# Folding the attention values into the three FFN weight matrices, with a written instruction order

## The chip, the cores and the metric

The kernel runs on one core of a Trainium2 chip. Its engines have instruction queues of their own and run beside each other: TensorE (PE in the profile; its weight loads are PEld), VectorE (DVE), ScalarE (ACT), GpSimd (POOL, which here mostly issues the loads) and SyncE (SP, which issues the stores). The metric is the device time of one execution in microseconds; lower is better.

## The reference

Batch 8, 8 heads, 576 tokens, head size 64, 32 memory slots; then a feed-forward network (FFN) of width 768 on all 8·576 = 4608 tokens of 512 channels. Inputs and output are float32.

```python
a = softmax(phi, axis=2)                      # per token, over 32 slots
k_m = einsum('bhsm,bhsd->bhmd', a, k)         # 32 x 64 per head
v_m = einsum('bhsm,bhsd->bhmd', a, v)
attn = softmax(0.125 * q @ k_m.T)             # 576 x 32 per head
x = concat_heads(attn @ v_m)                  # 4608 x 512
h = max(x @ w1, x @ w2, x @ w3)               # 4608 x 768
out = h @ w_out                               # 4608 x 512
```

Both kernels leave out the subtraction of the maximum before each exponential.

## The kernel before, in words

**Attention, one batch after another** (`attention_batch`). `load_batch` brings phi, k, v and q in with GpSimd's DMA queue, which also narrows them to bf16: per tensor four DMAs of two heads (`L121`, `L134`), in which a partition holds four neighbouring tokens, and a fifth for the last 64 tokens (`L127`, `L140`). ScalarE takes the exponential of phi (`L148`, `L155`); VectorE rearranges k and v into `kv_c` and q into `q_tc`. Then, for each of two groups of four heads and each of two pairs in it, TensorE contracts k and v over the tokens (`L210`), transposes q (`L234`) and the values (`L248`, `L254`), and forms the scores (`L292`) in a PSUM tile `stage`. The softmax over the 32 slots goes through three ScalarE steps on `stage`: exponential (`L300`), logarithm of the sums (`L317`, after a matmul that sums, `L309`), and the exponential of minus that (`L330`, after a matmul that spreads it, `L322`); VectorE multiplies (`L334`). Last, `L347` multiplies by the values, and `L354` writes the result transposed into `xT`, which holds all 4608 tokens in SBUF.

**The FFN, in 9 tiles of 512 tokens** (`ffn_tile`). For each of 6 slices of 128 of the 768 channels, 3 x 4 matmuls of 128x512 contract the 512 channels of x with w1, w2 and w3 (`L388`) into `acc01` (two PSUM banks) and `acc2`. ScalarE copies both to bf16 (`L396`, `L398`), VectorE takes the two maxima (`L400`, `L403`). Then 4 x 6 matmuls with w_out (`L410`), copies by ScalarE (`L418`) and stores by SP (`L427`).

A planner that knows costs puts the instructions of each engine in order; in the program's text attention stands ahead of the whole FFN, and the planner mixes the first FFN tiles into the attention. Each engine takes its instructions in that order, and semaphores hold an instruction until its inputs are there. PSUM has 8 banks of 2 KB per partition; `acc01`, `acc2` and `po2` each have one buffer.

Of the kernel before, what the change touches and what calls it, by code (L numbers as in the profile page):

```python
# [12 lines left out]

EXACT_SOFTMAX = True
# [3 lines left out]
def kernel(  # L19
# [17 lines left out]
    CMAIN = 4  # L37
    SMAIN = CMAIN * P
    TAIL = S - SMAIN
    NCH = CMAIN + 1  # L40
    csz = [P] * CMAIN + [TAIL]

    DM = H * D
    DF = moe_w1.shape[1]
    NTOK = B * S
    NPAIR = H // 2
    NGRP = H // 4
    CCH = DM // P
    FCH = DF // P
    NT = 512  # L50
    NTILES = NTOK // NT

    const_pool = ctx.enter_context(tc.tile_pool(name="const", bufs=1))
    w_pool = ctx.enter_context(tc.tile_pool(name="wpool", bufs=1))
    xt_pool = ctx.enter_context(tc.tile_pool(name="xt", bufs=1))
    batch_pool = ctx.enter_context(tc.tile_pool(name="batch", bufs=2))
    batch1_pool = ctx.enter_context(tc.tile_pool(name="batch1", bufs=1))
    grp_pool = ctx.enter_context(tc.tile_pool(name="grp", bufs=2))
    pair_pool = ctx.enter_context(tc.tile_pool(name="pairp", bufs=2))
    ffn_sb_pool = ctx.enter_context(tc.tile_pool(name="ffnsb", bufs=3))  # L60
    hT_pool = ctx.enter_context(tc.tile_pool(name="hT", bufs=2))

    pair_psum_pool = ctx.enter_context(tc.tile_pool(name="ppsum", bufs=1, space=bass.MemoryType.PSUM))
    stage_psum_pool = ctx.enter_context(tc.tile_pool(name="spsum", bufs=1, space=bass.MemoryType.PSUM))
    ffn_psum_pool = ctx.enter_context(tc.tile_pool(name="fpsum", bufs=1, space=bass.MemoryType.PSUM))

    AB0 = 0
    DEN0 = 64
    BF0 = 68
    VMT0 = 0  # L70
    QT0 = 64

    def bf16_view(ppsum):
        return ppsum[:, BF0:512].bitcast(BF16)

    ident = const_pool.tile([P, P], BF16, name="ident")
    make_identity(nc, ident)

    ones_diag4 = const_pool.tile([P, 4], BF16, name="ones_diag4")
    nc.gpsimd.memset(ones_diag4, 0.0)  # L80
    for g4 in range(4):
        nc.vector.memset(ones_diag4[32 * g4 : 32 * (g4 + 1), g4 : g4 + 1], 1.0)

    blkones = const_pool.tile([P, P], BF16, name="blkones")
    nc.gpsimd.memset(blkones, 1.0)
    nc.gpsimd.affine_select(
        out=blkones, in_=blkones, compare_op=ALU.is_ge,
        fill=0.0, base=0, pattern=[[1, P]], channel_multiplier=-M,
    )
    nc.gpsimd.affine_select(  # L90
        out=blkones, in_=blkones, compare_op=ALU.is_ge,
        fill=0.0, base=M - 1, pattern=[[-1, P]], channel_multiplier=M,
    )

    den_cols = const_pool.tile([P, 2], BF16, name="den_cols")
    nc.vector.memset(den_cols[:, 0:1], 1.0)
    nc.vector.memset(den_cols[:, 1:2], 32.0)

    w_tiles = [w_pool.tile([P, CCH, DF], BF16, name=f"w{wi}") for wi in range(3)]
    wot = w_pool.tile([P, FCH, DM], BF16, name="wot")  # L100

    def emit_weight_dmas(step):
        if step < 3:
            w_ap = (moe_w1, moe_w2, moe_w3)[step]
            src = w_ap.rearrange("(cc p) f -> p cc f", p=P)
            for cc in range(CCH):
                nc.gpsimd.dma_start(
                    out=w_tiles[step][:, cc], in_=src[:, cc]
                )
        elif step == 3:  # L110
            src = moe_w_out.rearrange("(fc p) c -> p fc c", p=P)
            for fc in range(FCH):
                nc.gpsimd.dma_start(out=wot[:, fc], in_=src[:, fc])

    xT = xt_pool.tile([P, NPAIR, NTOK], BF16, name="xT")

    def load_batch(b):
        bt = {}
        phi_t = batch1_pool.tile([P, H, NCH, M], BF16, name="phi_t")
        for hp in range(H // 2):  # L120
            nc.gpsimd.dma_start(  # L121
                out=phi_t[:, 2 * hp : 2 * hp + 2, 0:CMAIN, :],
                in_=phi[b, 2 * hp : 2 * hp + 2, 0:SMAIN, :].rearrange(
                    "h (p c) m -> p h (c m)", c=CMAIN
                ),
            )
        nc.gpsimd.dma_start(  # L127
            out=phi_t[0:TAIL, :, CMAIN, :],
            in_=phi[b, :, SMAIN:S, :].rearrange("h s m -> s h m"),
        )  # L130
        for name, src in (("k", k), ("v", v), ("q", q)):
            t = batch_pool.tile([P, H, NCH, D], BF16, name=f"{name}_t")
            for hp in range(H // 2):
                nc.gpsimd.dma_start(  # L134
                    out=t[:, 2 * hp : 2 * hp + 2, 0:CMAIN, :],
                    in_=src[b, 2 * hp : 2 * hp + 2, 0:SMAIN, :].rearrange(
                        "h (p c) d -> p h (c d)", c=CMAIN
                    ),
                )
# [46 lines left out]
    def attention_batch(b):  # L186
# [5 lines left out]
        for g in range(NGRP):  # L192
# [150 lines left out]
            for pp in range(2):  # L343
# [15 lines left out]
                )  # L359

    def out_segments(col0):
        segs = []
        col = col0
        while col < col0 + P:
            b = col // S
# [107 lines left out]
```

## Time and profile before

| what | value |
|---|---|
| time, median of 3 runs | 372.61 us (370.12 to 381.8) |
| profiled execution, first to last instruction (span) | 371.9 us |
| PE busy | 299.6 us, 81% |
| ACT busy | 203.4 us, 55% |
| DVE busy | 139.8 us, 38% |
| POOL busy | 139.4 us, 37% |
| read from HBM, written | 39.32 MB, 9.44 MB |

The profiled execution's own time is its span; the page gives no other, and the span lies 0.7 us under the median of the runs. Busy time of PE counts a matmul to its modelled end, which overlaps the start of the next, so it is no measure of peak rate. In a group's row stand the line, the engine, the operation, the tiles, the shape, the count, the busy time in us, the mean of one in ns, and the idle time ahead of them with what ended it. A matmul's row gives rows x columns of the array in use (`128*64`) and then the shape of the moving operand.

### The profile page before, as it was taken

The page shows a single profiled execution, that of the slowest core. Times are in us where ns is not written, and L with a number is a line of the kernel's source. Part 1 is how long each engine was busy: PE and PEld are TensorE (multiplying, and loading weights), DVE is VectorE, ACT ScalarE, POOL GpSimd, SP SyncE. Part 2 cuts the span into 40 slices and gives each one's busy share as a digit, 9 for nine tenths or more (in the row PEclk, how much of TensorE's full clock was granted, in tenths as well). Part 3 has the DMA queues.
Part 4 walks back from the last instruction along what each step waited for, and adds up shares of the span by engine and source line. Part 5 has one row for each costly group of instructions (what it writes and reads, how often), then busy time and mean ns, then how long its engine had stood idle before and what let it go on. Part 6 is the DMA issues. An engine that isn't in the chain of part 4 may idle for free.

```text
span 371.9 us, 4813 instructions
## 1 busy us (share of the span) xinstructions
PE 299.6 (81%) x1651; PEld 130.9 (35%) x1680; DVE 139.8 (38%) x450; ACT 203.4 (55%) x263; POOL 139.4 (37%) x236
## 2 busy tenths in 40 slices
PE   0146576878798887987897779999999999999972
PEld 0023233323343333333343423344444444444430
DVE  0456436336457456366465431221213222121310
ACT  2026645753967578287466784545454544544541
POOL 9987976774998799474000000000000000000000
PEclk9999999996999899599989999999999999999997
DMA  6999999999999999695120001303022040212204
GB/s 61 159 99 147 121 102 133 109 96 128 104 139 121 168 157 147 61 129 63 52 54 10 3 0 30 85 0 105 10 57 56 2 114 0 72 42 56 58 0 114
DMA packets 60728, 29.42 MB, mean 79 GB/s; under 512 B 29216, under 2 KB 56096, under 8 KB 60704
## 3 DMA queue, kind: packets, MB, share of 16 engines
q0 software_dynamic: 54304, 19.67, 48.1%
q1 hardware_dynamic: 6400, 9.44, 9.7%
q8 instruction: 13, 0.21, 0.2%
q14 instruction: 11, 0.09, 0.1%
HBM read 39.32 MB, written 9.44 MB: 131 GB/s over the span
## 4 chain that ended last, share of the span: by engine, by line
PE 59%; ACT 12%; issue 4%; DVE 4%; DMA 4%; POOL 3%; ACTq 0%; DVEq 0%; POOLq 0%
PE acc L388 33%; PE po L410 12%; ACT L317 3%; PE stage L347 3%; PE ppsum L210 3%; PE stage L292 2%; DVE attn_g L334 2%; DMA k_t<-in_k_dram 2%; ACT eln L330 2%; ACT lncs L317 2%; PE ppsum L234 2%; ACT L330 2%; DMA wot<-in_moe_w_out_dram 2%; PE stage L322 1%; ACT h L396 1%
## 5 line engine op out<-in xcount | busy, mean ns | idle before, releaser
L388 PE MATMUL acc<-xT,w 128*128 128x512 bf16 x626 | 165.2, 392 | 5.3 <-DMA w<-in_moe_w_dram 2.1
L388 PEld LDWEIGHTS <-w 128*128 128x128 bf16 x648 | 58.9, 98 | 80.0 <-issue 20.9
L396 ACT CAST h<-acc 128x1024 bf16<-128x1024 f32 x54 | 54.6, 1011 | 53.5 <-PE acc L388 53.5
L410 PE MATMUL po<-wot,hT 128*128 128x512 bf16 x209 | 59.0, 391 | 3.4 <-ACT ost L418 1.1
L400 DVE TENSOR_TENSOR mx<-h 128x512 bf16<-128x512 bf16 x54 | 22.8, 423 | 88.3 <-ACT h L396 88.0
L210 PE MATMUL ppsum<-e_t,kv_c 128*128 128x32 bf16 (+1 forms) x320 | 24.0, 187 | 20.5 <-DVE kv_c L165 16.6
L418 ACT COPY ost<-po 128x1024 f32<-128x1024 f32 x18 | 18.2, 1009 | 32.7 <-PE po L410 26.9
L398 ACT CAST h<-acc 128x512 bf16<-128x512 f32 x54 | 31.8, 590 | 7.1 <-PE acc L388 6.9
L403 DVE TENSOR_TENSOR hT<-mx,h 128x512 bf16<-128x512 bf16 x54 | 22.9, 424 | 23.2 <-ACT h L398 19.0
L354 ACT ACTIVATE xT<-stage 128x576 bf16<-128x576 f32 x32 | 20.9, 652 | 18.7 <-PE stage L347 18.3
L210 PEld LDWEIGHTS <-kv_c 128*128 128x128 bf16 (+1 forms) x320 | 18.3, 100 | 35.5 <-DVE kv_c L165 16.8
L410 PEld LDWEIGHTS <-hT 128*128 128x128 bf16 x216 | 19.7, 99 | 29.4 <-issue 6.0
L347 PE MATMUL stage<-attn_g,vm_sb 64*128 64x512 bf16 x64 | 16.2, 342 | 14.7 <-DVE attn_g L334 13.3
L317 ACT ACT_TABLE_LOAD x16 | 20.5, 1283 | 9.0 <-PE stage L309 8.9
L121 POOL DMA_DIRECT2D phi_t<-in_phi_dram x32 | 24.8, 831 | 1.3 <-DMA wot<-in_moe_w_out_dram 0.9
L262 DVE TENSOR_SCALAR vm_sb<-ppsum,recips 32x64 bf16<-32x64 bf16 x64 | 15.8, 247 | 24.2 <-PE ppsum L254 14.9
L134 POOL DMA_DIRECT2D q_t<-in_q_dram x32 | 24.0, 780 | 0.6 <-issue 0.5
L134 POOL DMA_DIRECT2D k_t<-in_k_dram x32 | 23.7, 827 | 0.0
L134 POOL DMA_DIRECT2D v_t<-in_v_dram x32 | 23.0, 747 | 0.7 <-issue 0.6
L234 PE MATMUL ppsum<-ident,q_tc 128*128 128x128 bf16 (+1 forms) x160 | 21.0, 248 | 2.2 <-DVE q_tc L176 1.7
L196 POOL MEMSET vm_sb<- 128x128 bf16 x16 | 4.0, 254 | 46.6 <-PE stage L347 46.6
L330 ACT ACT_TABLE_LOAD x14 | 18.0, 1283 | 4.8 <-PE stage L322 4.7
(53 smaller groups left out, 265.3 us busy)
## 6 DMA issues: line engine op xcount, KB each, us to landing
out_dram<-ost SPq DMA_DIRECT2D x80, 64.0 KB, 1.7
k_t<-in_k_dram POOLq DMA_DIRECT2D x32, 128.0 KB, 4.0
v_t<-in_v_dram POOLq DMA_DIRECT2D x32, 128.0 KB, 4.3
q_t<-in_q_dram POOLq DMA_DIRECT2D x32, 128.0 KB, 4.3
out_dram<-ost SPq DMA_DIRECT2D x32, 128.0 KB, 2.4
w<-in_moe_w_dram POOLq DMA_DIRECT2D x12, 192.0 KB, 4.8
phi_t<-in_phi_dram POOLq DMA_DIRECT2D x32, 64.0 KB, 3.1
wot<-in_moe_w_out_dram POOLq DMA_DIRECT2D x6, 128.0 KB, 5.6
```

The source lines that it names most:

```text
L121: nc.gpsimd.dma_start(out=phi_t[:, 2 * hp : 2 * hp + 2, 0:CMAIN, :], in_=phi[b, 2 * hp : 2 * hp + 2, 0:SMAIN, :].rearrange("h (p c) m -> p ...
L134: nc.gpsimd.dma_start(out=t[:, 2 * hp : 2 * hp + 2, 0:CMAIN, :], in_=src[b, 2 * hp : 2 * hp + 2, 0:SMAIN, :].rearrange("h (p c) d -> p h ( ...
L210: nc.tensor.matmul(ppsum[:, AB0 + a * M : AB0 + (a + 1) * M], lhsT=kv_c[0:r, c, h, :, :], rhs=e_t[0:r, c, h, :], start=(c == 0), stop=(c = ...
L234: nc.tensor.transpose(pbf[:, QT0 + c * P : QT0 + c * P + r], q_tc[0:r, c, hA : hA + 2, :], ident[0:r, 0:r],)
L317: nc.scalar.activation(out=lncs[0:4, :], in_=stage[0:4, 0:S], func=AF.Ln, scale=1.0 / 32.0,)
L330: nc.scalar.activation(out=eln, in_=stage[:, 0:S], func=AF.Exp, scale=-1.0)
L347: nc.tensor.matmul(psum_out[:, s0:s1], lhsT=vm_sb[pp * 2 * M : (pp + 1) * 2 * M, :], rhs=mov_g[pp * 2 * M : (pp + 1) * 2 * M, s0:s1], star ...
L388: nc.tensor.matmul(tgt, lhsT=w_tiles[w][:, cc, ft * P : (ft + 1) * P], rhs=xT[:, cc, n0 : n0 + NT], start=(cc == 0), stop=(cc == CCH - 1),)
L396: nc.scalar.copy(out=h01, in_=acc01)
L398: nc.scalar.copy(out=h2, in_=acc2)
L403: nc.vector.tensor_tensor(out=hT[:, ft, :], in0=mx, in1=h2, op=ALU.max)
L410: nc.tensor.matmul(po2[:, i * DM : (i + 1) * DM], lhsT=hT[:, fc, ns * P : (ns + 1) * P], rhs=wot[:, fc, :], start=(fc == 0), stop=(fc == F ...
```

## The change

Since x @ w = attn @ (v_m @ w) head by head, the kernel after multiplies the values into the weights first. For each batch and each slice of 128 channels, `fold` forms v_m @ w for 4 heads x 32 slots = 128 rows, in two groups, and `ffn1` contracts attn over these 2 x 128 slots, where the kernel before contracted x over 4 x 128 channels. `attn @ v_m` and `xT` are gone.

The data's layout changes with it. Two heads share the 128 partitions, 64 each, and each partition holds 9 neighbouring tokens of its head: one DMA per tensor and batch (4 instead of 20), with contiguous runs of 9 x 64 numbers. phi stays float32. The exponentials of phi go into a tile that is zero outside a head's own half (`e_bd`), k, v and a block of ones lie in one tile (`kvo`), and one matmul contracts all three (`att_kv`), in two column halves of the array by `tile_position`. Scores are formed in eight tiles of 64x32 of the array (`att_score`). One matmul with a block of ones sums and spreads (`att_norm`). `fold` too uses two column halves.

A table set for ScalarE is named at the start. The maxima read PSUM directly, the first of them against `h1`, the copy of the first product. Two PSUM pools stay: `acc` with two buffers of two banks (scores, sums and FFN1 share it), `one` with four of one bank. The order is written out by hand: batch 0 goes through attention and FFN and batch 1 through attention, one step after another; from then on FFN1 of batch b, in 18 pieces, is mixed with FFN2 of batch b-1 and with the attention and folding of batch b+1, each put ahead of the piece whose number stands beside it.

```diff
--- before.py
+++ after.py
...
+    nc.scalar.preload_act_table_set("natural_log_exp_and_others")
+    ident = const.tile([P, P], BF16, name="ident")
...
+    blkones = const.tile([P, P], BF16, name="blkones")
+    nc.vector.memset(blkones, 0.0)
+    for i in range(P // M):
+        nc.vector.memset(blkones[M * i : M * (i + 1), M * i : M * (i + 1)], 1.0)
+    ones2 = const.tile([P, 2], BF16, name="ones2")
+    nc.vector.memset(ones2, 1.0)
+    e_bds, vm_bds, kvos = [], [], []
+    for i in range(2):
+        e_bd = const.tile([P, NP, NC, 2, M], BF16, name=f"e_bd{i}")
+        nc.vector.memset(e_bd, 0.0)
+        e_bds.append(e_bd)
+        vm_bd = const.tile([P, NP, 2, M], BF16, name=f"vm_bd{i}")
+        nc.vector.memset(vm_bd, 0.0)
+        vm_bds.append(vm_bd)
+        kvo = const.tile([P, 3, NP, NC, D], BF16, name=f"kvo{i}")
+        nc.vector.memset(kvo[:, 2], 1.0)
+        kvos.append(kvo)
...
+    def load(b):
+        t = {}
+        ph = inp.tile([P, NP, NC, M], FP32, name="ph")
+        kv = kvos[b % 2]
+        qq = inp.tile([P, NP, NC, D], BF16, name="qq")
+        def go(dst, src, n):
+            s = src[b].rearrange("h s d -> (h s) d").rearrange(
+                "(j p c) d -> p j (c d)", p=P, c=NC
+            )
+            nc.gpsimd.dma_start(out=dst.rearrange("p j c d -> p j (c d)"), in_=s)
+        go(ph, phi, M)
+        go(kv[:, 0], k, D)
+        go(kv[:, 1], v, D)
+        go(qq, q, D)
+        t["ph"], t["kv"], t["q"] = ph, kv, qq
+        loaded[b] = t
...
+    def att_exp(b):
+        s = st.setdefault(b, {})
+        ph = loaded[b]["ph"]
+        e_bd = e_bds[b % 2]
+        for a in range(2):
+            r = slice(HP * a, HP * (a + 1))
+            nc.scalar.activation(out=e_bd[r, :, :, a, :], in_=ph[r], func=AF.Exp)
+        s["e"] = e_bd
+    def att_kv(b, g):
+        s = st[b]
+        if g == 0:
+            s["kvp"] = one_pool.tile([P, NG, 3 * D], FP32, name="kvp", tag="one")
+        kv, e_bd, kvp = loaded[b]["kv"], s["e"], s["kvp"]
+        for c in range(NC):
+            for i in range(2):
+                j = 2 * g + i
+                nc.tensor.matmul(
+                    kvp[HP * i : HP * (i + 1), g, :],
+                    lhsT=e_bd[:, j, c],
+                    rhs=kv[:, :, j, c, :],
+                    start=(c == 0),
+                    stop=(c == NC - 1),
+                    tile_position=(0, HP * i),
+                )
+    def att_kv_norm(b):
+        s = st[b]
+        kvp = s["kvp"]
+        rden = work.tile([P, NG], FP32, name="rden")
+        nc.vector.reciprocal(out=rden, in_=kvp[:, :, 2 * D])
+        kvn = work.tile([P, NG, 2 * D], BF16, name="kvn")
+        for g in range(NG):
+            nc.vector.tensor_scalar_mul(
+                out=kvn[:, g], in0=kvp[:, g, 0 : 2 * D], scalar1=rden[:, g : g + 1]
+            )
+        s["kvn"] = kvn
+    def att_kv_t(b):
+        s = st[b]
+        kvt = one_pool.tile([P, NP, 2, M], BF16, name="kvt", tag="one")
+        for g in range(NG):
+            nc.tensor.transpose(kvt[:, 2 * g : 2 * g + 2], s["kvn"][:, g], ident)
+        kmT = work.tile([P, NP, 2, M], BF16, name="kmT")
+        for u in range(2):
+            nc.vector.tensor_copy(out=kmT[HP * u : HP * (u + 1)], in_=kvt[0:HP])
+        vm_bd = vm_bds[b % 2]
+        for a in range(2):
+            nc.vector.tensor_copy(
+                out=vm_bd[HP * a : HP * (a + 1), :, a, :], in_=kvt[HP:P, :, a, :]
+            )
+        s.update(kmT=kmT, vm=vm_bd)
+    def att_q(b, jj):
+        s = st[b]
+        qq = loaded[b]["q"]
+        if jj == 0:
+            s["qT"] = work.tile([P, NP, NCP, P], BF16, name="qT")
+        qT = s["qT"]
+        x = b % 2
+        if jj < NP // 2:
+            pt = one_pool.tile([P, 2, NCP - 1, P], BF16, name="pt", tag="one")
+            for i in range(2):
+                for c in range(NCP - 1):
+                    nc.tensor.transpose(
+                        pt[:, i, c, :], qq[:, 2 * jj + i, 2 * c : 2 * c + 2, :], ident
+                    )
+            nc.vector.tensor_copy(
+                out=qT[:, 2 * jj : 2 * jj + 2, x : x + NCP - 1, :], in_=pt
+            )
+        else:
+            pt = one_pool.tile([P, NP, P], BF16, name="pt", tag="one")
+            for j in range(NP):
+                nc.tensor.transpose(pt[0:HP, j, :], qq[:, j, NC - 1, :], ident)
+            nc.vector.tensor_copy(
+                out=qT[0:HP, :, 0 if x else NCP - 1, :], in_=pt[0:HP]
+            )
+    def att_score(b, g):
+        s = st[b]
+        kmT, qT = s["kmT"], s["qT"]
+        x = b % 2
+        if g == 0:
+            s["e2"] = work.tile([P, NG, S + HP], BF16, name="e2")
+            s["attn"] = work.tile([P, NG, S], BF16, name="attn")
+        sc = acc_pool.tile([P, 2, BANK], FP32, name="sc", tag="acc")
+        for par in range(2):
+            nch = NCP - par
+            c0 = x * par
+            r = slice(HP * par, HP * (par + 1))
+            for h4 in range(4):
+                j, a = 2 * g + h4 // 2, h4 % 2
+                nc.tensor.matmul(
+                    sc[M * h4 : M * (h4 + 1), par, 0 : nch * HP],
+                    lhsT=kmT[r, j, a, :],
+                    rhs=qT[r, j, c0 : c0 + nch, HP * a : HP * (a + 1)],
+                    start=True,
+                    stop=True,
+                    tile_position=(HP * par, M * h4),
+                )
+        for par in range(2):
+            nch = NCP - par
+            nc.scalar.activation(
+                out=s["e2"][:, g].rearrange("p (c u n) -> p c u n", u=2, n=HP)[
+                    :, 0:nch, par, :
+                ],
+                in_=sc[:, par, 0 : nch * HP].rearrange("p (c n) -> p c n", n=HP),
+                func=AF.Exp,
+                scale=0.125,
+            )
+    def att_norm(b, g):
+        s = st[b]
+        e2 = s["e2"]
+        sm = acc_pool.tile([P, 2, BANK], FP32, name="sm", tag="acc")
+        for h in range(2):
+            nc.tensor.matmul(
+                sm[:, h, 0:SH],
+                lhsT=blkones,
+                rhs=e2[:, g, h * SH : (h + 1) * SH],
+                start=True,
+                stop=True,
+            )
+        ln = work.tile([P, S], FP32, name="ln")
+        nc.scalar.activation(
+            out=ln.rearrange("p (h n) -> p h n", h=2),
+            in_=sm[:, :, 0:SH],
+            func=AF.Ln,
+        )
+        r = work.tile([P, S], FP32, name="r")
+        nc.scalar.activation(out=r, in_=ln, func=AF.Exp, scale=-1.0)
+        nc.vector.tensor_tensor(
+            out=s["attn"][:, g, :], in0=e2[:, g, 0:S], in1=r, op=ALU.mult
+        )
+    def fold(b, ft):
+        s = st[b]
+        if ft == 0:
+            s["wp"] = work.tile([P, NG, FT, 3, P], BF16, name="wp")
+        for g in range(NG):
+            wps = one_pool.tile([P, 3, P], FP32, name="wps", tag="one")
+            for i in range(2):
+                nc.tensor.matmul(
+                    wps[HP * i : HP * (i + 1)],
+                    lhsT=s["vm"][:, 2 * g + i],
+                    rhs=w_sb[:, 2 * g + i, :, ft * P : (ft + 1) * P],
+                    start=True,
+                    stop=True,
+                    tile_position=(0, HP * i),
+                )
+            if g == 0:
+                nc.scalar.copy(out=s["wp"][:, g, ft], in_=wps)
+            else:
+                nc.vector.tensor_copy(out=s["wp"][:, g, ft], in_=wps)
+    def ffn1(b, ft, w):
+        s = st[b]
+        if (ft, w) == (0, 0) and b % 2 == 0:
+            hts[b // 2] = work.tile([P, FT, 2 * S], BF16, name="hT")
+        hT = hts[b // 2]
+        acc = acc_pool.tile([P, 2, BANK], FP32, name="acc", tag="acc")
+        for g in range(NG):
+            for h in range(2):
+                nc.tensor.matmul(
+                    acc[:, h, 0:SH],
+                    lhsT=s["wp"][:, g, ft, w, :],
+                    rhs=s["attn"][:, g, h * SH : (h + 1) * SH],
+                    start=(g == 0),
+                    stop=(g == NG - 1),
+                )
+        a = acc[:, :, 0:SH]
+        if w == 0:
+            s["h1"] = hpool.tile([P, 2, SH], BF16, name="h1")
+            nc.scalar.copy(out=s["h1"], in_=a)
+        elif w == 1:
+            h2 = hpool.tile([P, 2, SH], BF16, name="h2")
+            nc.vector.tensor_tensor(out=h2, in0=a, in1=s["h1"], op=ALU.max)
+            s["h2"] = h2
+        else:
+            nc.vector.tensor_tensor(
+                out=hT[:, ft, (b % 2) * S : (b % 2 + 1) * S].rearrange("p (h n) -> p h n", h=2),
+                in0=a,
+                in1=s["h2"],
+                op=ALU.max,
+            )
+    def ffn2(b, t):
+        hT = hts[b // 2]
+        po = one_pool.tile([P, DM], FP32, name="po", tag="one")
+        c0 = S - HP if t == 4 else (b % 2) * (S + HP) + t * P
+        for fc in range(FT):
+            nc.tensor.matmul(
+                po,
+                lhsT=hT[:, fc, c0 : c0 + P],
+                rhs=wo_sb[:, fc, :],
+                start=(fc == 0),
+                stop=(fc == FT - 1),
+            )
...
+    def ffn2_tiles(b):
+        return 4 if b % 2 == 0 else 5
+    load(0)
+    load_w(0)
+    load_w(1)
+    load_wo()
+    load(1)
+    def attention(b):
+        att_exp(b)
+        for g in range(NG):
+            att_kv(b, g)
+        att_kv_norm(b)
+        for jj in range(3):
+            att_q(b, jj)
+        att_kv_t(b)
+        for g in range(NG):
+            att_score(b, g)
+        for g in range(NG):
+            att_norm(b, g)
+    attention(0)
+    for ft in range(FT):
+        fold(0, ft)
+        for w in range(3):
+            ffn1(0, ft, w)
+    for t in range(ffn2_tiles(0)):
+        ffn2(0, t)
+    load(2)
+    attention(1)
+    for ft in range(FT):
+        fold(1, ft)
+    for b in range(1, B):
+        fill = []
+        if b >= 2:
+            n = ffn2_tiles(b - 1)
+            for t in range(n):
+                fill.append((18.0 * (t + 0.5) / n, lambda t=t: ffn2(b - 1, t)))
+        if b + 1 < B:
+            c = b + 1
+            fill.append((4.0, lambda: att_exp(c)))
+            for g in range(NG):
+                fill.append((6.0 + g, lambda g=g: att_kv(c, g)))
+            fill.append((7.5, lambda: att_kv_norm(c)))
+            for jj in range(3):
+                fill.append((8.0 + jj, lambda jj=jj: att_q(c, jj)))
+            fill.append((9.5, lambda: att_kv_t(c)))
+            fill.append((11.5, lambda: att_score(c, 0)))
+            fill.append((12.5, lambda: att_score(c, 1)))
+            fill.append((14.0, lambda: att_norm(c, 0)))
+            fill.append((15.0, lambda: att_norm(c, 1)))
+            for ft in range(FT):
+                fill.append((11.8 + 1.05 * ft, lambda ft=ft: fold(c, ft)))
+        if b + 2 < B:
+            fill.append((10.9, lambda: load(b + 2)))
+        fill.sort(key=lambda x: x[0])
+        for i in range(18):
+            while fill and fill[0][0] <= i:
+                fill.pop(0)[1]()
+            ffn1(b, i // 3, i % 3)
+        for _, f in fill:
+            f()
+    for t in range(ffn2_tiles(B - 1)):
+        ffn2(B - 1, t)
...
-    def attention_batch(b):
...
-    def ffn_tile(nt):
...
-    for b in range(B):
-        attention_batch(b)
-        if 1 <= b <= 4:
-            emit_weight_dmas(b - 1)
-    for nt in range(NTILES):
-        ffn_tile(nt)
```

More of the change, by code (lines that the diff above doesn't have):

```diff
@@ L13 @@
 ALU = mybir.AluOpType
-EXACT_SOFTMAX = True
 @with_exitstack
@@ L55 @@
[L55 to L63, printed above, removed]
@@ L80 @@
[L80 to L93, printed above, removed]
@@ L95 @@
[L95 to L108, printed above, removed]
-                )
[L110 to L113, printed above, removed]
@@ new lines, in load_w, with load_wo @@
+    def load_w(half):
+        n = DF // 2
+        for i, w in enumerate((moe_w1, moe_w2, moe_w3)):
+            nc.gpsimd.dma_start(
+                out=w_sb[:, :, i, half * n : (half + 1) * n],
+                in_=w.rearrange("(j p) f -> p j f", p=P)[:, :, half * n : (half + 1) * n],
+            )
+    def load_wo():
+        nc.gpsimd.dma_start(
+            out=wo_sb, in_=moe_w_out.rearrange("(t p) c -> p t c", p=P)
+        )
+    st = {}
+    def att_exp(b):
[6 more added lines that the diff above has]
+        s["e"] = e_bd
```

357 lines of the change are left out of this document (41 added, 316 removed).

## The prediction

> **What bounds the kernel now.** First the page: busy time, the slices with PE's clock and the DMA share, the loads' queue, the chain that ended last.
>
> ```profile
> PE 299.6 (81%) x1651; PEld 130.9 (35%) x1680; DVE 139.8 (38%) x450; ACT 203.4 (55%) x263; POOL 139.4 (37%) x236
> PE   0146576878798887987897779999999999999972
> DMA  6999999999999999695120001303022040212204
> q0 software_dynamic: 54304, 19.67, 48.1%
> PE acc L388 33%; PE po L410 12%; ACT L317 3%; PE stage L347 3%; PE ppsum L210 3%; PE stage L292 2%; DVE attn_g L334 2%; DMA k_t<-in_k_dram 2%; ACT eln L330 2%; ACT lncs L317 2%; PE ppsum L234 2%; ACT L330 2%; DMA wot<-in_moe_w_out_dram 2%; PE stage L322 1%; ACT h L396 1%
> ```
>
> Two stages are seen. Up to about 186 us the loads fill the DMA engines (9 in nearly every slice) and PE is busy in part; from 228 us PE is at 9 throughout. The windows (busy us and instructions by engine, then clock, DMA share, GB/s written) and PE's timeline and groups say what each runs at:
>
> ```profile
> 0.00:186.00 186.00, 132.03 (x860) 59.52 (x874) 89.52 (x315) 105.62 (x140) 138.35 (x230) 0.94 0.99 115
> 228.00:372.00 144.00, 132.82 (x575) 56.42 (x585) 30.61 (x72) 67.58 (x86) 0.00 (x0) 0.99 0.20 52
> 236.80 2.75 PE L388 MATMUL acc<-xT,w 128*128 128x512 bf16 x12
> ...
> L388 PE MATMUL acc<-xT,w 128*128 128x512 bf16 x418 | 98.1, 379 | 1.7 <-ACT h L396 0.7
> ...
> L388 PE MATMUL acc<-xT,w 128*128 128x512 bf16 x14 | 7.5, 622 | 2.5 <-DMA w<-in_moe_w_dram 2.1 <-issue 0.3
> ```
>
> Twelve matmuls take 2.75 us, the last of them 0.379: one per (2.75 - 0.379)/11 = 0.2155 us, or 0.421 ns a column. The FFN's 648 + 216 matmuls at that rate are 186 us, half of the span, with nothing left to squeeze but the work itself. The last two rows are the groups of 230 to 360 us and of 40 to 77 us: 379 against 622 ns for one matmul, so before 77 us PE ran at about half rate, although the page's clock row shows 9 there (its first event comes later). I count the start of the new kernel at half clock too.
>
> **The change, per batch, from durations of before.**
>
> ```profile
> L396 ACT CAST h<-acc 128x1024 bf16<-128x1024 f32 x54 | 54.6, 1011 | 53.5 <-PE acc L388 53.5
> L398 ACT CAST h<-acc 128x512 bf16<-128x512 f32 x54 | 31.8, 590 | 7.1 <-PE acc L388 6.9
> L403 DVE TENSOR_TENSOR hT<-mx,h 128x512 bf16<-128x512 bf16 x54 | 22.9, 424 | 23.2 <-ACT h L398 19.0
> L285 DVE COPY qT_sb<-ppsum 128x576 bf16<-128x576 bf16 x32 | 14.6, 457 | 1.0
> L334 DVE TENSOR_TENSOR attn_g<-exp_g,eln 128x576 bf16<-128x576 bf16 x16 | 12.1, 757 | 20.1 <-ACT eln L330 20.1
> L330 ACT ACTIVATE eln<-stage 128x576 f32<-128x576 f32 x16 | 10.4, 648 | 1.6 <-PE stage L322 1.5
> L148 ACT ACTIVATE e_t<-phi_t 128x512 bf16<-128x512 bf16 x16 | 9.7, 625 | 14.7 <-DMA phi_t<-in_phi_dram 14.7
> L241 DVE CAST vmT_sb<-ppsum 64x32 bf16<-64x32 f32 x32 | 6.2, 194 | 28.2 <-PE ppsum L234 28.0
> ...
> 167.50 0.44 PE L292 MATMUL stage<-qT_sb,kmT_sb 128*64 128x512 bf16 x4
> 167.87 0.38 PE L210 MATMUL ppsum<-e_t,kv_c 128*128 128x32 bf16 x5
> ...
> 169.91 0.53 PE L234 MATMUL ppsum<-ident,q_tc 128*128 128x128 bf16 x5
> ...
> 178.51 0.43 PE L292 MATMUL stage<-qT_sb,kmT_sb 128*64 128x512 bf16 x2
> ```
>
> *PE.* FFN1: 72 matmuls of 288 columns, 72 x 288 x 0.421 ns = 8.7 us (before 81 x 0.2155 = 17.5). FFN2 unchanged: 27 x 0.2155 = 5.8. Folding: 24 matmuls of 384 columns in two column halves. Do halves overlap? L292 answers: one half's two matmuls (512 and 64 columns) took 0.43 us, both halves' four 0.44. So 12 pairs x 0.162 = 1.9 us. `att_kv`: 18 pairs of 192 columns, 0.081 each = 1.5; with a floor of 0.05 per step (L210: 5 in 0.38, the last some 0.19) 36 x 0.05 = 1.8; I take 1.7. Transposes: L234's 5 in 0.53 give 0.08 each, 22 of them 1.8. Scores: eight tiles at once aren't shown; from all at once (0.14 us a group) to one by one (0.97); near L292, taken as 0.25, so 0.5. Sums: 4 x 288 columns = 0.5.
>
> Changes of array shape cost extra:
>
> ```profile
> 166.98 0.59 PE L388 MATMUL acc<-xT,w 128*128 128x512 bf16 x2
> ```
>
> The second of these began at 167.19 and would have let a like one start at 167.41; L292's came at 167.50, 0.09 us late. I count 20 changes per batch (folding 12 with what it shares with the scores, the rest `att_kv`, scores, odd transposes): 1.8 us. PE in all: 8.7 + 5.8 + 1.9 + 1.7 + 1.8 + 0.5 + 0.5 + 1.8 = 22.7 us.
>
> The Trainium skill, "TensorEngine Tiling (Array Packing)", section Tiling Modes (Key Properties), speaks against the change here: another tiling mode drains the array. By that a change would cost the whole tail of a matmul, 0.379 - 0.2155 = 0.16 us from the rows above, and the sum 24.1; the trace has 0.09.
>
> *ACT.* L396 and L398 give 0.169 us + 0.822 ns a column from PSUM; L148 0.204 us to start from SBUF. Exponentials of phi 2 x 1.15; of scores 2 x (0.43 + 0.38); logarithm and exponential 2 x (0.65 + 0.68); folded weights 6 x 0.485; `h1` 6 x 0.648; FFN2's copies 4.5 x 0.59: 16.1 us. The copies into `xT` and the two big FFN copies are gone; the table loads I count as gone too, all but one, since one set is named at the start:
>
> ```profile
> L317 ACT ACT_TABLE_LOAD x16 | 20.5, 1283 | 9.0 <-PE stage L309 8.9
> L330 ACT ACT_TABLE_LOAD x14 | 18.0, 1283 | 4.8 <-PE stage L322 4.7
> ```
>
> *DVE.* The maxima now read float32 from PSUM, which no row shows: between L403's rate (0.475 for 576) and L334, which has one float32 input as they have (0.757); I take the latter: 12 x 0.757 = 9.1. Folded weights 6 x 128x384: 0.36 at L285's rate, 0.56 at L334's; taken 0.56, 3.3. Copies of q and of the slots by L285 and L241 (0.19 us + 0.48 ns a column) 1.8 + 1.1; `att_kv_norm` 0.75; L334's multiply 2 x 0.757. Sum 17.6 us, 13 at the low ends.
>
> *Loads.* 4.13 MB per batch are read as before, in 4 DMAs with runs twice as long. Row q0: 48.1% of 371.9 = 179 us for 54304 packets of 362 bytes; the longer ones are cheaper a byte. The best stretch of loading:
>
> ```profile
> 10.00:20.00 10.00, 1.17 (x15) 0.86 (x15) 4.80 (x10) 0.00 (x0) 10.00 (x18) 1.00 1.38 154
> 12.37 1.29 DVE L165 COPY kv_c<-k_t 128x1024 bf16<-128x1024 bf16 x2 [10.91 <-DMA k_t<-in_k_dram]
> 15.76 1.40 DVE L165 COPY kv_c<-v_t 128x1024 bf16<-128x1024 bf16 x2 [1.53 <-DMA v_t<-in_v_dram]
> ```
>
> 154 GB/s written is 308 read: 13.4 us a batch; at the mean 115 it is 18. Stores add about 4.5 (9.44 of 29 MB). Both fit under the loop below, and POOL, with 39 DMAs left of 178, runs ahead: no bound, but it sets the start.
>
> *Waits that come in.* A product of FFN1 waits until the product two before it has been read: for `h1` by ACT, behind which may stand phi's exponentials (2.3 us at piece 4), else by DVE. Behind the waiting matmul stands all of PE's queue, and behind DVE's first maximum, which waits for `h1`, stand the copies of q, the slots and the folded weights that PE's next steps need. *Taken at nothing:* VectorE's fillings at the start, four of 2304 numbers, at L334's rate 2.4 us each and 10 us in all, beside the loads that take until 14; were that cover gone, 10 us. The stores: SP issues two per batch beside the loop, where before 112 went beside the FFN.
>
> **The sum.** *Start.* k of batch 0 landed at 12.4 us, v at 15.8; with the longer runs I take 14 for v, 18 for q. Then one long chain, since batch 0 overlaps with nothing: `att_kv` at half clock to 17.5, transposes and copies to 22, scores, two exponentials, logarithm, exponential per group (4.3 us on ACT) and the multiply to 28. The weights (6.3 MB at 308 GB/s) are in by 39, w1 to w3 by 33, hidden. FFN1 of batch 0 has nothing beside it: per slice, fold, copy (0.56), first product and `h1` (0.3 + 0.17 + 0.65), two maxima (1.5), at full clock 3.3 us, six at some 3.5 = 21: 49. FFN2 5 to 8: 56. Attention of batch 1 again a chain (2.3 for phi, whose exponential stands behind FFN2's copies on ACT; 14 more) and folding 3: 75 us.
>
> *Loop, b = 2 to 6.* PE 22.7, DVE 17.6, ACT 16.1: PE bounds. But the fixed order isn't even: from piece 12 to 16 ACT has exponentials 1.6, logarithms 2.65, five folded copies 2.4, `h1` 1.3, FFN2 0.9 = 8.9 us against PE's 8.4, and the products, scores and sums share two buffers, so that a late ACT stops PE. The handovers there are shown nowhere: from nothing (rival 1) to a whole busy spell of ACT behind PE's (rival 2); I put them at 2.3 us, nearer to nothing, since a buffer is back 0.17 + 0.65 us after its product and the loop gives a piece 1.25 us on average: 25 a batch, 5 x 25 = 125. *b = 1* lacks FFN2 (-4.7): 20. *b = 7* has 18 pieces and four tiles: PE 13.9, with two buffers 14.5. *End*: wait for the last maximum 0.9, five tiles 6.5, then copy and stores:
>
> ```profile
> 365.05 1.01 ACT L418 COPY ost<-po 128x1024 f32<-128x1024 f32 x1 [2.84 <-PE po L410]
> ```
>
> Before, 5.8 us passed after that copy, with 12 DMAs to issue; now two, 2.5: 10 in all. Sum: 75 + 20 + 125 + 14.5 + 10 = **244 us**, against the span of 371.9; the runs' median is 0.7 above the span, which I leave out of the sum as it is far below its other doubts.
>
> **Rivals.**
> 1. *PE alone decides* (0.17): ACT's crowding is absorbed. 70 + 18 + 5 x 22.7 + 14 + 10 = 225 us. For it: from 228 us on PE held 132.8 of 144 us with ACT at 68 beside it. Against it: there ACT and DVE had a third of the work that the loop gives them.
> 2. *The order stalls* (0.20): the two shared buffers and in-order queues add 6 us more a batch, as if ACT's and DVE's busiest spells fell one behind the other. 75 + 25 + 5 x 31 + 17 + 10 = 282. For it: in the interleaved stage before, PE waited often (132 of 186 us).
> 3. *It doesn't do what it says: the table loads stay* (0.06), two per group, 4 x 1.283 = 5.1 us a batch on ACT in its crowded spell: 244 + 6 x 5.1 = 275. Or *column halves don't pay* (0.06) because their weight loads, 36 in `att_kv` and 24 in `fold`, don't hide: 1.9 + 1.5 us twice over, 270. L292 speaks against it.
> 4. *Slower: half clock throughout* (0.04). The array's 20.9 us of a batch double, plus 1.8 and 2.3: 46; 82 + 35 + 5 x 46 + 29 + 17 = 393. It decides from about 86% of the time at half clock ((372 - 244) / (393 - 244)). For it: the 622 ns above, in a mixed stage, and what went ahead of two later spells:
>
> ```profile
> 81.10:84.50 3.40, 1.29 (x7) 1.00 1.18 130
> 84.50:91.30 6.80, 6.39 (x30) 0.50 0.97 135
> 146.00:149.30 3.30, 2.18 (x18) 1.00 1.37 145
> 149.30:159.60 10.30, 9.83 (x46) 0.50 0.70 62
> ```
>
> (PE's busy us and matmuls, clock, DMA.) PE busy 1.29 of 3.4 us, and 2.18 of 3.3, was followed by half clock for 7 and 10 us. Against it: the loop keeps PE at 22.7/25 = 91%, and both spells ended by themselves. The Trainium skill, "TensorE: Matmul & The Clock Gate" (What's actually happening), lets the clock drop only after an idle window of some 3.4 us; by that this rival would fall, since no wait that I find in the loop is so long. The trace doesn't agree: PE did work in both windows.
>
> **How the numbers follow.** Forecast 244 (232 to 258) 0.46, rivals 0.17, 0.20, 0.12, 0.04, and 0.01 for no change. A measurement of this kernel tells about 2% from nothing. The range from 216 (rival 1 with a start of 61) to 290 (rivals 2 and 3 at their ends) leaves out about 0.15. Faster 0.95, same 0.01, slower 0.04.
>
> **What would show it.** A first FFN1 product of batch 1 near 75 us, then periods of 25; PE over 85% in 100 to 220 us; maxima near 757 ns, folded copies near 560; one ACT_TABLE_LOAD; column halves starting together; matmuls of 288 columns 0.121 apart. I am wrong if the loop waits for ACT or DVE through whole batches, or loads land after attention asks for them.

## The result

| | before | after |
|---|---|---|
| median of the runs, us | 371.37 (368.35 to 381.8) | 257.10 (254.93 to 258.09) |
| span of the profiled run, us | 371.9 | 253.2 (its time 254.93) |

The ratio of after to before is 0.693 (95% interval 0.686 to 0.701): 114 us less. The ratio leaves out the slow run of 381.8 us, which is more than 1.5% above the fastest of its kernel. The forecast was 244 us, the range 216 to 290.

The page of the kernel after, the lines that answer to those of before: busy time, PE's and the DMA's slices, the loads' queue, the chain.

```profile
PE 195.2 (77%) x1589; PEld 111.0 (44%) x1608; DVE 139.1 (55%) x252; ACT 121.5 (48%) x213; POOL 29.9 (12%) x45
PE   0176878586797889889788998897988998888970
...
DMA  5999999999469205991397639950001500720177
q0 software_dynamic: 17776, 22.02, 47.4%
PE 47%; DVE 24%; ACT 18%; issue 4%; DMA 3%; POOL 1%; DVEq 0%; POOLq 0%
```

PE's busy time fell by 104 us, ACT's by 82 and POOL's by 110; DVE's stayed where it was. But PE is mostly at 7 to 9 tenths and not at 9 throughout, and the chain that ended last is only 47% PE's. The loads' time (47.4% of 253 us is 120 us, before 179) is less, for a third of the packets.

One of the 18 pieces of a batch's FFN1 is called a product here; it is four matmuls of 288 columns. A loop is the time from one batch's first product to the next batch's. The windows that follow are these loops (columns as in the prediction); the last one runs from batch 7's first product to the end:

```profile
63.30:88.60 25.30, 19.96 (x176) 11.57 (x175) 15.70 (x30) 12.43 (x23) 2.97 (x4) 0.89 0.61 112
88.60:115.20 26.60, 23.65 (x201) 13.48 (x204) 16.67 (x31) 15.14 (x28) 2.98 (x4) 1.00 0.66 129
...
195.00:221.60 26.60, 23.70 (x204) 13.55 (x206) 16.72 (x31) 15.32 (x28) 0.00 (x0) 1.00 0.35 79
221.60:253.20 31.60, 21.77 (x125) 12.04 (x126) 9.93 (x14) 9.28 (x16) 0.00 (x0) 0.95 0.37 84
```

All five full loops take 26.6 us, to the tenth. No engine is busy for all of one: PE 23.7 by modelled ends, DVE 16.7, ACT 15.3. Where PE stands still inside a loop, its timeline shows (start, length, count; in brackets PE's idle time and who ended it). In the loop from 141.8 us these waits add up to 2.6 us; the two longest and the first that follows ACT's block are:

```profile
148.57 0.93 PE L139 MATMUL kvp<-kvo,e_bd 128*64 128x192 bf16 x18 [0.17 <-ACT e_bd L128]
...
157.15 0.32 PE L214 MATMUL sc<-qT,kmT 64*32 64x320 bf16 x8 [0.88 <-DVE h L301]
...
164.52 0.65 PE L288 MATMUL acc<-attn,wp 128*128 128x288 bf16 x4 [0.80 <-ACT ln L246]
```

The first follows phi's exponentials (ACT, 2.33 us in one block), the second DVE's spell of copies, the third the logarithms. The order written by hand puts each spell into a few pieces; whether it is this order that costs the time, the experiments have to show.

### The profile page after: what moved, and what is told of

Read it like the earlier page. It is cut to its first block, busy times and chain, and to the rows that moved or that the text cites. A ratio compares the mean times of both kernels' runs of the same rounds, so it can differ in the third digit from the quotient of the medians.

```text
span 253.2 us, 3962 instructions
## 1 busy us (share of the span) xinstructions
PE 195.2 (77%) x1589; PEld 111.0 (44%) x1608; DVE 139.1 (55%) x252; ACT 121.5 (48%) x213; POOL 29.9 (12%) x45
## 3 DMA queue, kind: packets, MB, share of 16 engines
q0 software_dynamic: 17776, 22.02, 47.4%
## 4 chain that ended last, share of the span: by engine, by line
PE 47%; DVE 24%; ACT 18%; issue 4%; DMA 3%; POOL 1%; DVEq 0%; POOLq 0%
PE acc L288 19%; PE po L319 14%; DVE h L301 6%; ACT e_bd L128 6%; PE kvp L139 6%; DVE hT L304 6%; PE wps L264 5%; ACT ln L246 4%; DVE qT L189 3%; ACT h L298 3%; DMA kvo<-in_v_dram 3%; ACT r L252 3%; DVE kvn L155 2%; DVE wp L275 2%; DVE kmT L167 1%
## 5 line engine op out<-in xcount | busy, mean ns | idle before, releaser
L288 PE MATMUL acc<-attn,wp 128*128 128x288 bf16 x576 | 93.4, 295 | 17.4 <-ACT ln L246 4.8
L288 PEld LDWEIGHTS <-wp 128*128 128x128 bf16 x576 | 53.4, 99 | 52.9 <-issue 27.1
L301 DVE TENSOR_TENSOR h<-acc,h 128x576 bf16<-128x576 f32 x48 | 36.2, 754 | 50.4 <-PE acc L288 36.3
L319 PE MATMUL po<-wo_sb,hT 128*128 128x512 bf16 x197 | 48.2, 379 | 1.5 <-issue 0.5
L298 ACT CAST h<-acc 128x576 bf16<-128x576 f32 x48 | 30.6, 638 | 36.1 <-PE acc L288 35.7
L304 DVE TENSOR_TENSOR hT<-acc,h 128x576 bf16<-128x576 f32 x48 | 36.3, 756 | 8.3 <-PE acc L288 5.2
L329 ACT COPY ost<-po 128x512 f32<-128x512 f32 x32 | 18.7, 585 | 40.6 <-PE po L319 40.5
L275 DVE CAST wp<-wps 128x384 bf16<-128x384 f32 x48 | 26.2, 551 | 12.3 <-PE wps L264 12.0
L139 PE MATMUL kvp<-kvo,e_bd 128*64 128x192 bf16 x288 | 16.0, 264 | 19.7 <-DMA kvo<-in_v_dram 11.6
L273 ACT CAST wp<-wps 128x384 bf16<-128x384 f32 x48 | 22.9, 479 | 11.9 <-PE wps L264 11.6
L264 PE MATMUL wps<-w_sb,vm_bd 128*64 128x384 bf16 x192 | 26.0, 352 | 2.6 <-ACT wp L273 1.9
L128 ACT ACTIVATE e_bd<-ph 64x1152 bf16<-64x1152 f32 x16 | 18.6, 1161 | 4.0 <-DMA ph<-in_phi_dram 3.9
## 6 DMA issues: line engine op xcount, KB each, us to landing
wo_sb<-in_moe_w_out_dram POOLq DMA_DIRECT2D x1, 768.0 KB, 18.6
```

Source lines behind the costliest of these rows:

```text
L128: nc.scalar.activation(out=e_bd[r, :, :, a, :], in_=ph[r], func=AF.Exp)
L139: nc.tensor.matmul(kvp[HP * i : HP * (i + 1), g, :], lhsT=e_bd[:, j, c], rhs=kv[:, :, j, c, :], start=(c == 0), stop=(c == NC - 1), tile_p ...
L264: nc.tensor.matmul(wps[HP * i : HP * (i + 1)], lhsT=s["vm"][:, 2 * g + i], rhs=w_sb[:, 2 * g + i, :, ft * P : (ft + 1) * P], start=True, s ...
L273: nc.scalar.copy(out=s["wp"][:, g, ft], in_=wps)
L275: nc.vector.tensor_copy(out=s["wp"][:, g, ft], in_=wps)
L288: nc.tensor.matmul(acc[:, h, 0:SH], lhsT=s["wp"][:, g, ft, w, :], rhs=s["attn"][:, g, h * SH : (h + 1) * SH], start=(g == 0), stop=(g == N ...
```

## The experiments

**Theory A**: part of the loop's 26.6 us are handovers; PE has less work than that, and stands still behind ACT's and DVE's spells and the two product buffers because of where the written order puts things. **Theory B**: PE's work fills the loop and I priced it too low.

Runs 3, 8, 11 and 12 are medians of four executions. The others are one execution each, and the four of the kernel after lie up to 3.2 us apart; so the length of the loops, of which five in a row can be compared, says more than the time.

**1. Twice the contraction.** FFN1 adds each of its products twice.

```diff
-        for g in range(NG):
+        for gg in range(2 * NG):
+            g = gg % NG
...
-                    start=(g == 0),
-                    stop=(g == NG - 1),
+                    start=(gg == 0),
+                    stop=(gg == 2 * NG - 1),
```

> Each FFN1 product contracts its 256 slots twice, 8 matmuls instead of 4, as many as a contraction over 512 channels; the result is then twice the product. PE gets 8.7 us more per batch. Theory A (handovers: PE stands still for about 4 us of the loop's 26.6, behind ACT's and DVE's crowded spells and the two buffers): part of the 8.7 fills those waits, loop 31 to 33 us, span 290 to 305. Theory B (PE's own work fills the loop, and I priced it too low): loop 35.3, span about 320.

```profile
133.80:166.70 32.90, 31.01 (x273) 20.04 (x272) 16.68 (x31) 14.90 (x27) 2.97 (x4) 1.00 0.47 87
```

Loops of 32.8 and 33.3 us, time 305.5: of 8.7 us added, 6.5 show. The other 2.2 went into time in which PE had stood still. That is as A has it, at the upper end of its 31 to 33. The run also says what the halved contraction is worth here: with as many matmuls as a contraction over 512, the kernel would be 48 us slower.

**2. Less FFN2.** One matmul of six per tile in batches 1 to 6.

```diff
-        for fc in range(FT):
+        n2 = 1 if 1 <= b < B - 1 else FT
+        for fc in range(n2):
...
-                stop=(fc == FT - 1),
+                stop=(fc == n2 - 1),
```

> FFN2 of batches 1 to 6 does one of its six matmuls per tile (output wrong for those), copies and stores stay: PE has 4.9 us less per loop. A: the chain over ACT and DVE stays, loop 25 to 25.6 us, as batch 1's loop without FFN2 took 25.3. B: loop 21.7, span about 228.

```profile
115.50:139.30 23.80, 18.63 (x181) 11.27 (x180) 16.37 (x30) 14.65 (x27) 2.98 (x4) 1.00 0.59 111
139.30:164.30 25.00, 20.16 (x180) 11.48 (x181) 16.34 (x30) 15.22 (x28) 2.98 (x4) 0.93 0.89 180
```

Time 242.3. The loops at full clock took 23.7 to 23.8, between A's 25 to 25.6 and B's 21.7, so both were off: 2.9 of 4.9 us came off and 2.0 did not. Two other loops took 25.0 and 25.2, with a spell at half clock in each. PE was busy for 18.6 us by modelled ends and still the loop took 23.8; I read that as the chain over the other engines, which no run here takes away. So neither theory holds alone: PE's work and the waits for the others share the loop.

**3. A third product buffer.** It is taken from the single banks.

```diff
-        tc.tile_pool(name="accp", bufs=2, space=bass.MemoryType.PSUM)
+        tc.tile_pool(name="accp", bufs=3, space=bass.MemoryType.PSUM)
...
-        tc.tile_pool(name="onep", bufs=4, space=bass.MemoryType.PSUM)
+        tc.tile_pool(name="onep", bufs=2, space=bass.MemoryType.PSUM)
```

> Three buffers of two banks for products, scores and sums, and two instead of four single banks. A, if the two buffers are the main wait: loop 24.5 to 25.5, span 243 to 248. A, if it is ACT's and DVE's queues themselves: loop within 0.5 of 26.6. B: no change. If two single banks are too few for folding and FFN2: loop longer, 28.

```profile
149.35 2.15 PE L288 MATMUL acc<-attn,wp 128*128 128x288 bf16 x16
...
158.09 1.47 PE L319 MATMUL po<-wo_sb,hT 128*128 128x512 bf16 x6 [0.71 <-DVE kvn L155]
...
171.03 0.35 PE L264 MATMUL wps<-w_sb,vm_bd 128*64 128x384 bf16 x2 [1.21 <-DVE wp L275]
```

Time 258.8, loops of 26.9 to 27.2 (one of 28.5 with half clock). Sixteen matmuls, four products, now run without a wait (2.15 us, 0.12 each), but PE waits for the single banks, of which only two are left (the waits for `kvn` and `wp` in the last two rows). The two pools share eight banks (2 x 2 + 4, here 3 x 2 + 2), so this run doesn't price the product buffers by themselves.

**4. The planner's order.** The same instructions, in the order that the planner gives them.

```diff
-    ctx.enter_context(tc.manual_schedule())
```

> The same instructions, but the planner orders each engine's queue instead of the written order. A: order decides, so the loop moves by over 1 us one way or the other; if the planner fills PE's waits better, span 235 to 245, if it sends ACT or DVE astray, over 270. B: within 2% of 253.

```profile
106.80:130.10 23.30, 23.28 (x202) 13.35 (x201) 16.54 (x31) 14.95 (x27) 2.22 (x3) 1.00 0.56 102
...
129.66 0.60 PE L318 MATMUL po<-wo_sb,hT 128*128 128x512 bf16 x2
130.10 0.65 PE L287 MATMUL acc<-attn,wp 128*128 128x288 bf16 x4
130.59 0.81 PE L318 MATMUL po<-wo_sb,hT 128*128 128x512 bf16 x3
131.24 0.65 PE L287 MATMUL acc<-attn,wp 128*128 128x288 bf16 x4
```

Time 231.5, loops of 23.3 to 23.4 after a first one of 22.2, PE busy for 23.28 of 23.3. This settles A against B: the same work fits into 23.3 us, and 3.3 us of each loop were the written order. The timeline shows one means: FFN2's matmuls mostly go one to three at a time between the products, where the written order has six in one block. The kernel is some 25 us slower in the written order, which is a part of the change, than in the planner's; by the spans it is 23.5, of which the five full loops make 17.3 and the loop of batch 1 makes 3.3.

**5 to 7. Which places in the written order.** Run 5 gives out phi's exponentials in two halves, apart from each other.

```diff
-            fill.append((4.0, lambda: att_exp(c)))
+            fill.append((0.9, lambda: att_exp(c, (0,))))
+            fill.append((3.9, lambda: att_exp(c, (1,))))
```

Run 6 gives out each FFN2 tile in three parts of two matmuls.

```diff
-                fill.append((18.0 * (t + 0.5) / n, lambda t=t: ffn2(b - 1, t)))
+                for part in range(3):
+                    fill.append((18.0 * (t + (part + 0.5) / 3) / n,
+                                 lambda t=t, part=part: ffn2(b - 1, t, part)))
```

Run 7 does both, and spreads the projection of q.

```diff
-                fill.append((8.0 + jj, lambda jj=jj: att_q(c, jj)))
+                fill.append((1.0 + 2 * jj, lambda jj=jj: att_q(c, jj)))
```

> Written order; the two halves of phi's exponential for the next batch stand ahead of pieces 1 and 4 instead of both ahead of piece 4. Theory A1 (ACT's block of 2.3 us there holds up the key and value contraction, and VectorE's crowded spell then starts late): loop 25 to 26 us, span 244 to 250. Rival A2 (PE stands still because whole FFN2 tiles, six matmuls each, leave the other pieces with nothing between two products): loop 26.6, no change.

> Written order; every FFN2 tile is given out in three parts of two matmuls, spread evenly over the pieces. A2: loop 24 to 25.3 us, span 238 to 246. A1: loop 26 to 26.6.

> Written order with both of these and q's transposes and copies ahead of pieces 1, 3 and 5 instead of 8, 9 and 10. If the order's places are all that divides the loop from the planner's 23.3 us: 23.3 to 24.3, span 234 to 240. If the planner's gain needs more (exponentials a batch ahead, other places of the folding): 24.8 or more.

Run 5, run 6 and two loops of run 7:

```profile
138.60:164.90 26.30, 23.55 (x203) 13.50 (x204) 16.66 (x31) 15.25 (x28) 2.97 (x4) 1.00 0.83 170
...
141.10:167.00 25.90, 23.43 (x203) 13.58 (x205) 16.74 (x31) 14.86 (x27) 2.97 (x4) 1.00 0.85 173
...
136.00:160.50 24.50, 22.99 (x201) 13.34 (x204) 16.79 (x31) 14.87 (x28) 2.98 (x4) 1.00 0.88 182
160.50:184.60 24.10, 22.65 (x197) 12.84 (x199) 16.30 (x31) 14.77 (x27) 0.00 (x0) 1.00 0.06 14
```

Run 5 (time 250.2): 25.6 and 26.3 in turn, over the five loops 0.55 less in the mean. Run 6 (249.8): 25.9, 0.7 less, where A2 expected 24 to 25.3. A1 comes out nearest, with its 25 to 26 and 26 to 26.6 each missed by about 0.1 or less in the mean, but the two moves gain about the same, so neither place alone is the cause. Run 7: 24.3 in the mean, 2.3 less (time 240.5). Three small moves took two thirds of the 3.3 us; the last 1.0 is not traced to a place. The gains of the two that were tried alone add up to 1.25, so 1.0 of run 7's 2.3 belongs to q's places or to the three moves together; no run moves q alone.

**8, 11, 12. The end and the start, on the planner's order.** Run 8 stores each FFN2 tile of the last batch as it is copied, run 11 those of the last two (`b >= B - 2`).

```diff
-            if t == 3:
+            if b == B - 1:
+                rows = out[b * S : (b + 1) * S, :].rearrange("(p c) d -> p c d", c=NC)
+                for u in range(2):
+                    par = (u + b) % 2
+                    nc.sync.dma_start(
+                        out=rows[:, par + 2 * t, :],
+                        in_=osts[b][HP * u : HP * (u + 1), t],
+                    )
+            elif t == 3:
```

Run 12 is run 11 and begins the mixed loop with batch 0.

```diff
-        for w in range(3):
-            ffn1(0, ft, w)
-    for t in range(ffn2_tiles(0)):
-        ffn2(0, t)
-    load(2)
-    attention(1)
-    for ft in range(FT):
-        fold(1, ft)
...
-    for b in range(1, B):
+    for b in range(0, B):
...
-        if b >= 2:
+        if b >= 1:
```

> Planner's order, and in the last batch each FFN2 tile is stored as soon as it is copied, 64 KB x 2 a tile, instead of 512 KB x 2 after the fourth. If the end is the stores' transfer of 1.25 MB in 7 us: end after the last copy 3 us instead of 7, span 225 to 227. If the end is the fixed way of a store: 229.7 as without.

> Planner's order; the last two batches store each FFN2 tile as it is copied. If the end waits for 2.3 MB of stores of both batches at some 206 GB/s (11 us from the first store on): end 2.5 to 4 us after the last copy instead of 6.1 with the last batch alone, span 224 to 226. If SP's issuing of the many DMAs is the limit: 228 or more.

> As before it, and the mixed loop begins with batch 0: batch 1's attention is given out among batch 0's FFN1, FFN2 of batch 0 goes into batch 1's loop. If loads allow it (q of batch 1 lands at some 45 us): first product of batch 1 at 55 instead of 62.4, one fuller loop of 23.3 instead of 22, span 217 to 222. If batch 1's loads come late or the planner had mixed them already: 223 to 226.

The last copies (ACT, start and length) of the kernel after, of run 8, run 11 and run 12, whose spans are 253.2, 228.4, 226.3 and 224.2 us:

```profile
245.41 0.58 ACT L340 COPY ot<-po 128x512 f32<-128x512 f32 x1 [0.71 <-PE po L319]
...
221.69 0.58 ACT L347 COPY ot<-po 128x512 f32<-128x512 f32 x1 [0.71 <-DMA out_dram<-ost]
...
221.49 0.59 ACT L347 COPY ot<-po 128x512 f32<-128x512 f32 x1 [0.71 <-PE po L318]
...
219.37 0.59 ACT L347 COPY ot<-po 128x512 f32<-128x512 f32 x1 [0.71 <-PE po L318]
```

From the last copy's end to the span's: 7.2 us, 6.1, 4.2, 4.2 (in run 4, on the planner's order alone, 7.2 too). Run 8 gave 1.1 of the expected 4: SP issued the last stores only at 224.4, 2.1 us after the copy, as it was still busy with the stores ahead of them, 1 MB of the batch before among them. With both batches spread out (run 11) they were issued 0.1 us after the copy, and the end is 4.2, still above the expected 2.5 to 4. Times: run 8 230.5 us, run 11 228.4, run 12 226.1. The last step brought 2 us, with a first product of batch 1 at 60.2 and a span of 224.2, which is the second of its two forecasts (223 to 226). Run 12 is the fastest version found: 0.613 of before (0.609 to 0.617), 12% less than the kernel after.

**9 and 10. The table set.** This one line taken out of the kernel after (9), and that line alone put into the kernel before (10).

```diff
-    nc.scalar.preload_act_table_set("natural_log_exp_and_others")
```

> The kernel after in its written order, without the table set named at the start. If the set is what keeps table loads away (the prediction's rival 3): 32 or more loads of 1.28 us, 5.1 us a batch more on ACT, in the spell where ACT already holds PE up: loop 30 to 32 us, span 280 to 295. If ACT's waits elsewhere hide them: loads appear, span below 265. If one set is kept anyway: one load, 253.

> The kernel before with only this one part of the change, the table set named at the start: 33 loads fall to 1, 41 us less on ACT. By the chain of before (table loads 5% of the span) 350 to 360 us; if the loads there were beside PE's work and the DMA, within 2% of 372.

Groups of run 9, one of its loops, and the chain by line of run 10:

```profile
L245 ACT ACT_TABLE_LOAD x16 | 20.5, 1283 | 0.3
L251 ACT ACT_TABLE_LOAD x16 | 20.5, 1283 | 0.3
...
138.50:170.50 32.00, 24.13 (x200) 13.70 (x199) 16.32 (x30) 19.84 (x31) 2.97 (x4) 0.95 0.45 84
...
PE acc L389 36%; PE po L411 13%; PE ppsum L211 2%; PE ppsum L235 2%; PE stage L348 1%; PE stage L293 1%; PE stage L323 1%; PE stage L310 1%; ACT ost L419 1%; ACT h L397 1%; PE ppsum L221 1%; PE ppsum L249 0%; DVE attn_g L335 0%; DVE vm_sb L263 0%; ACT lncs L318 0%
```

Run 9: 301.6 us, 44 more than after and above the forecast of 280 to 295, for 32 loads more, 41 us of ACT's time. Some 33 us of them lie in the chain that ended last. The loops of 32.0 and 32.9 us are 5.4 to 6.3 longer than those of the kernel after. In the first of them three of the four loads lie in the chain, 3.8 us; the rest goes with spells at half clock (clock 0.95 and 0.90) behind the longer waits, as where PE stood still for 3.9 us behind the logarithm. Run 10: 351.9 us, 5% less than before, with one table load left of 33, and none in its chain, which can be followed back to 132 us.

## Why the prediction was right, and where it was off

The direction, its size and the range held. The sum, term by term:

| term | forecast | measured |
|---|---|---|
| start, to batch 1's first product | 75 | 63.3 |
| loop b = 1 | 20 | 25.3 |
| five loops | 125 | 133.0 |
| b = 7 and end | 24.5 | 31.6 |

Four terms were off by 5 to 12 us, and one had the other sign, so 11.7 us too many in the start made up for more than half of the 20.4 too few in the others. That the forecast came within 13 us of the time is in part luck.

*PE's work, 22.7 us a batch*: right to 3%; the planner's loop needs 23.3. The 0.121 us a matmul (16 in 2.15) and the overlap of column halves held. The eight tiles of the scores, which no row of before showed, ran all at once: 0.32 us for the eight in the row at 157.15, where one alone has a mean of 0.31. The durations held too:

```profile
L301 DVE TENSOR_TENSOR h<-acc,h 128x576 bf16<-128x576 f32 x48 | 36.2, 754 | 50.4 <-PE acc L288 36.3 <-ACT h L298 13.6
L275 DVE CAST wp<-wps 128x384 bf16<-128x384 f32 x48 | 26.2, 551 | 12.3 <-PE wps L264 12.0
L273 ACT CAST wp<-wps 128x384 bf16<-128x384 f32 x48 | 22.9, 479 | 11.9 <-PE wps L264 11.6
L128 ACT ACTIVATE e_bd<-ph 64x1152 bf16<-64x1152 f32 x16 | 18.6, 1161 | 4.0 <-DMA ph<-in_phi_dram 3.9
```

(means 754, 551, 479, 1161 ns; forecast 757, 560, 485, 1150).

*The handovers, put at 2.3 us*: mis-sized; 3.9 by the same PE sum (26.6 - 22.7). I had named ACT's spell at the late pieces; DVE's spell of copies between pieces 8 and 12, behind which the scores waited 0.88 us, was in my list of waits but not in the sum.

*"b = 1 lacks FFN2 (-4.7)"*: the step that failed. It takes the loop for PE's, where PE's work comes off in full. Run 2 took 4.9 us off and gained 2.9 at full clock; and b = 1, with a clock of 0.89 in its window, ran at half clock for 5.5 us of its 25.3 besides. The 4.7 itself has no source: by the prediction's own rate the four tiles of batch 0 are 24 x 0.2155 = 5.2, and 25 - 4.7 is 20.3.

*Start*: too long by 11.7. v landed at 11.6 us, not 14, and from there to FFN1 of batch 0 passed 10.5 us, not 14: it began at 22.0, not 28. VectorE's fillings, put at 10 us and beside the loads, took 6.0 and were over at 9.1. The six slices of batch 0's FFN1 took 20, forecast 21, and its FFN2 6.1 instead of 7. Batch 1's attention and folding took 15 after the last FFN2 copy, not 19, since folding began at 57.8 while the last group's logarithms still ran:

```profile
11.57 2.94 PE L139 MATMUL kvp<-kvo,e_bd 128*64 128x192 bf16 x36 [11.57 <-DMA kvo<-in_v_dram]
...
22.04 0.66 PE L288 MATMUL acc<-attn,wp 128*128 128x288 bf16 x2 [1.28 <-ACT wp L273]
...
57.82 0.84 PE L264 MATMUL wps<-w_sb,vm_bd 128*64 128x384 bf16 x8
```

*b = 7 and end*: the stores after the last copy took 7.2 us, not 2.5. I counted DMAs to issue, not the 1 MB that the fourth tile sets free at once, with 0.25 MB of the fifth behind it. Batch 7's pieces took 18.2 us up to the last maximum's end at 239.8, forecast 14.5 + 0.9; the planner's order took 16.3 for them.

*Rivals*: the first (PE alone) is what the planner's order does, and run 11 (228.4) came near its 225. The second, that the order stalls, was the right mechanism at half its size: 3.9 us over PE's sum, where it had 8.3. The third's table loads came true only when the line was taken out. Half clock showed in the start, in b = 1 and, in runs 2, 3 and 9, in full loops, but never throughout.

What the runs leave open: of the parts of the change only the halved contraction, the table set and the order were undone one at a time. What the layout of the data, the column halves and the maxima that read PSUM directly give of the 114 us, no run separates.

## What to carry to other kernels

Work taken from an engine shortens a loop in full only if that engine fills the loop. Before a written order is kept, run the same instructions in another order, such as the planner's, and compare the loops. Give out fill work in small parts between the instructions that wait for buffers, and spread each engine's spells; judge such moves together as well as one by one, since here two of them gave 1.25 us and the three 2.3. Before a sum, look for costs that repeat across the kernel and that one line removes: one named table set was worth 18.5 us before the change and 44 after it, where the halved contraction was worth 48.

## What the runs showed of the hardware that was not expected

PE's clock fell to half though PE worked in the window ahead. Two pairs of neighbouring windows of run 2 (PE's busy us come first, the clock stands ahead of the DMA share):

```profile
102.90:106.30 3.40, 1.66 (x20) 0.87 (x18) 3.21 (x8) 0.89 (x3) 0.75 (x1) 1.00 1.21 206
106.30:109.70 3.40, 3.40 (x23) 1.03 (x21) 0.82 (x3) 2.31 (x6) 0.00 (x0) 0.50 1.22 212
...
120.00:123.40 3.40, 1.82 (x28) 1.26 (x29) 1.11 (x2) 1.77 (x3) 0.76 (x1) 1.00 0.04 8
123.40:126.80 3.40, 3.40 (x50) 2.85 (x48) 1.86 (x5) 0.98 (x3) 1.48 (x2) 1.00 0.71 180
```

PE was busy for 1.66 of 3.4 us while DVE made its copies, and then ran 3.4 us at half clock; the two loops with such a spell took 25.0 and 25.2 us instead of 23.7. The full loops of the kernel after, with more work on PE, had no such spell. So removing PE's work can lengthen the rest of it. The Trainium skill, "TensorE: Matmul & The Clock Gate" (What's actually happening), names an idle window for this; here, as in the prediction's rows, the window was half busy. PE's busy time alone does not decide it: after 1.82 of 3.4 us the clock stayed at 1.00 in the second pair, and after 2.18 of 3.3 us it fell in the prediction's rows. What does decide it, no run tells.
